# Three steps of a single-core FNet and ReGLU kernel moved later, and the first rounding of a transform block given to GpSimd

## The chip, the core and the metric

The kernel runs on one core of a Trainium2 chip. The core has five engines with a queue of instructions each: TensorE (PE, with its weight loads shown apart as PEld), VectorE (DVE), ScalarE (ACT), GpSimd (POOL) and SyncE (SP, which here only issues transfers). They meet through semaphores. The metric is the device time of one execution in microseconds (us). Before the change it is 1030.93 us, the median of 3 runs (1029.65 to 1031.65).

## What is computed

`x` is 2048 tokens by 640 features. The rows are normalized, and the result is the sum of the input, a two-dimensional Fourier transform of the normalized rows (its real part, by matrices) and a gated feed-forward layer with 1728 hidden units:

```python
xn = _layernorm(x, axis=-1)
# A: Fourier mixing
a = jnp.einsum("bsd,ed->bse", xn, dft_hid_re)
b = jnp.einsum("bsd,ed->bse", xn, dft_hid_im)
A = jnp.einsum("ts,bse->bte", dft_seq_re, a) - jnp.einsum("ts,bse->bte", dft_seq_im, b)
# B: gated layer
gate = jnp.einsum("bsd,df->bsf", xn, W_gate)
up = jnp.einsum("bsd,df->bsf", xn, W_up)
h = gate * (gate > 0) * up
B = jnp.einsum("bsf,fd->bsd", h, W_down)
return x + A + B
```

## The kernel before

**Products.** Every float32 operand is split in two parts that TensorE can take at its full rate: a rounded high part and a low remainder. The high part is a copy with a rounding output type, mostly made by ScalarE; the low part is the operand minus its high part, made by VectorE or GpSimd (`split`, L123 to L125). A product of two operands is three matmuls of 128x128 weights by 512 columns: high by high, high by low, low by high (`mm3`, L130 to L132). Where a block scheme with 7 products in place of 8 can be used, sums and differences of blocks are formed first; this is what names such as B11, T1 or S2 stand for.

**Stages.** The first stage (to about 400 us) normalizes the tokens and multiplies them by the sequence transform, whose blocks of 128x1024 stream in from memory. The second (405 to 722 us by its first and last weights) computes the gate and the up projection. The third multiplies by the hidden transform and by `W_down`, adds the input and stores (`project`).

**Work lists.** The first and the third stage are lists of units, each with four steps: load, prepare, run and finish. `drive(4, 2)` walks over the list and issues, at step i, the preparation of unit i-2, the load of unit i, the finish of unit i-5 and the matmuls of unit i-4. The order in which an engine gets its instructions follows from this walk and from a scheduler; instructions that pass through `pin` keep the order of the program. Each queue runs strictly in order, so an instruction that waits holds up all that stands behind it on its engine.

**The start.** A token group is 256 tokens, two to a partition (j = 0 and 1). `first_group` (L287) does group 0 by halves so that TensorE can begin early. 48 small matmuls on zeros (L112) keep TensorE busy while data arrive. The transfer of the x rows of j = 0 comes first, then the transform block `raw` of column chunk c = 0, then that of c = 1. VectorE takes mean and variance (L204, L205), ScalarE the square root (L210), VectorE its inverse (L210). `high(0, 0)` (L303, recorded at L292) is the ScalarE copy that rounds the first 128x512 block of `raw` into `cb`. Then come the high parts of the normalized tokens, columns 0 to 127 first (L231), and VectorE's low parts (L235). `behind_vector` (L248) is a one-column GpSimd multiply that reads the last of VectorE's low parts; it only puts GpSimd's next step behind it in time. That step, `low(0, 0, nc.gpsimd)` (L293), is the low part of the first `raw` block.

`first_products` (L502 on, recorded at L510) issues the matmuls of group 0 in this order for each j: high by high for c = 0, the tokens' low parts for c = 0, both for c = 1, and at the end the matmuls that take the low parts of the transform, c = 0 ahead of c = 1. So 12 matmuls stand ahead of the first one that needs GpSimd's L293.

**The other groups.** `next_group` (L250) does groups 1 to 7. For groups 1 to 3 its last VectorE step scales the columns that are kept in float32 (L276, two instructions), and `keep_a21` has GpSimd's queue store them. In the list, the split of the transform block for c = 1 of the running group is recorded right behind (L570, at L124 and L125), held there by `issue_after`. For group 4 (g equal to NH), ScalarE rounds both token halves (L231), and then copies three accumulators out of PSUM (`keep_first`, L593 on, at L121), which frees the next matmuls of chunk 0.

**The third stage's loads.** `get_y` (L1206) loads the blocks of x to which the results are added. `project` records it behind the unit u = 3 of each product; for B11 it loads three blocks (L1211) on SP's queue, between the loads of units 3 and 4.

Of the kernel before, what the change touches and what calls it, by code (L numbers as in the profile page):

```python
# [10 lines left out]
OP = mybir.AluOpType  # L11
# [8 lines left out]
SG = 2  # L20
# [38 lines left out]
def fnet_reglu_kernel(  # L59
# [43 lines left out]

    root_t = keep.tile([P, 1], F32, name="root_t")
    nc.scalar.activation(root_t, eps_t, AF.Sqrt)

    warm = keep.tile([P, P], mybir.dt.bfloat16, name="warm")
    nc.vector.memset(warm, 0.0)
# [121 lines left out]
    def ln_high(g, xs, mv, j, cs):  # L230
        return nc.scalar.activation(ln_parts(g, j, cs)[0], xs[:, j, cs], AF.Copy, scale=mv[:, j, 4:5])  # L231
# [10 lines left out]
    def pin(steps):  # L242
        return [tc.keep_in_program_order(i) for i in steps]
# [6 lines left out]
    def next_group(g, b, raw, before):  # L250

        xs, bs, mv = ln_tiles(g)
        js = slice(0, SG)
        cs = K14 if g < NH else slice(0, D)
        low = lambda engine, j: pin([engine.tensor_tensor(flat(b, 1)[:, j], raw[:, j], flat(b, 0)[:, j].bitcast(F32), op=OP.subtract)])
        pin(ln_stats(g, xs, bs, mv, js))
        pin([nc.scalar.activation(flat(b, 0), raw, AF.Copy)])
        if before is not None:
            behind_vector(before)
            for j in range(SG):  # L260
                low(nc.gpsimd, slice(j * CH, (j + 1) * CH))
        root, inverse = ln_first(g, mv, js)
        pin([root])
        pin([ln_mean(g, mv, js)])
        pin([ln_center(xs, mv, 0, cs)])
        pin([inverse()])
        pin([ln_high(g, xs, mv, 0, cs)])
        pin([ln_center(xs, mv, 1, cs)])
        late["high"] = pin([ln_high(g, xs, mv, 1, cs)])[0].ins
        if before is None:  # L270
            for j in range(SG):
                low(nc.vector, slice(j * CH, (j + 1) * CH))
        pin(ln_refine(g, mv, js))
        late["ln"] = pin(ln_low(g, xs, j, cs) for j in range(SG))[-1].ins
        if g < NH:
            late["ln"] = pin(nc.vector.tensor_scalar(xs[:, j, K2], xs[:, j, K2], mv[:, j, 0:1], stat[:, 1, g, j : j + 1],  # L276
                                                     op0=OP.subtract, op1=OP.mult) for j in range(SG))[-1].ins
            keep_a21(g)
        if g == NG - 1:
            nc.sync.dma_start(rows.rearrange("m (g p j) -> p m g j", p=P, j=SG), stat)  # L280
        if g == 2:
            st = stage()[:, :CH].rearrange("p (j d) -> p j d", j=SG)
            for j in range(SG):
                late["high"] = pin([nc.scalar.activation(st[:, j], ln_place(0)[:, j, K2], AF.Copy, scale=stat[:, 1, 0, j : j + 1])])[0].ins
            keep_a21(0, st)

    def first_group(b):  # L287


        xs, bs, mv = ln_tiles(0)  # L290
        part = lambda c, j: b[c][1][:, j * CH : (j + 1) * CH]
        high = lambda c, j: pin([nc.scalar.activation(b[c][0][:, 0, j], part(c, j), AF.Copy)])  # L292
        low = lambda c, j, engine: pin([engine.tensor_tensor(b[c][0][:, 1, j], part(c, j), b[c][0][:, 0, j].bitcast(F32),  # L293
                                                             op=OP.subtract)])
        d0, d14 = slice(0, P), slice(P, 3 * P)
        last = lambda j: ln_parts(0, j, K14)[1][:, 3 * P - 1 :]
        j0, j1 = slice(0, 1), slice(1, 2)
        pin(ln_stats(0, xs, bs, mv, j0))
        root, inverse = ln_first(0, mv, j0)
        pin([root])  # L300
        pin([ln_center(xs, mv, 0, d0)])
        pin([inverse()])
        high(0, 0)  # L303
        pin([ln_high(0, xs, mv, 0, d0)])
        pin([ln_center(xs, mv, 0, d14)])
        pin([ln_high(0, xs, mv, 0, d14)])
        pin(ln_refine(0, mv, j0))
        high(1, 0)
        pin(ln_low(0, xs, 0, cs) for cs in (d0, d14))
        behind_vector(last(0))  # L310
        low(0, 0, nc.gpsimd)

        low(1, 0, nc.vector)
        pin(ln_stats(0, xs, bs, mv, j1))
        high(0, 1)
        root, inverse = ln_first(0, mv, j1)
        pin([root])
        pin([ln_center(xs, mv, 1, K14)])
        pin([inverse()])
        pin([ln_high(0, xs, mv, 1, K14)])  # L320
        pin(ln_refine(0, mv, j1))
        high(1, 1)
        pin([ln_low(0, xs, 1, K14)])
        behind_vector(last(1))
        low(0, 1, nc.gpsimd)
        low(1, 1, nc.gpsimd)
        pin([ln_mean(0, mv, slice(0, SG))])
        for j in range(SG):
            pin([nc.scalar.activation(xs[:, j, K2], xs[:, j, K2], AF.Identity, bias=stat[:, 0, 0, j : j + 1])])
# [203 lines left out]
    def first_stream(c, name, g):  # L533

        t = {}
        half = int(name == "B21")
        n = half * NH + g

        norm = {0: 0 if n == 0 else None, 1: n + 1 if n < NG - 1 else None}.get(c)

        def load():
            if n == 0 and c == 0:
                st = start["raw"] = [raw(), raw()]
                get = lambda c, j: nc.sync.dma_start(st[c][:, j * CH : (j + 1) * CH], dft[c, 0, 0][:, j * CH : (j + 1) * CH])
                ln_load(0, slice(0, 1))
                get(0, 0)
                get(1, 0)
                ln_load(0, slice(1, 2))
                get(0, 1)
                get(1, 1)  # L550
                return
            if norm is not None:
                tc.keep_in_program_order(ln_load(norm, slice(0, SG)))
            if n > 0 or c > 1:
                t["s"] = raw()
                nc.sync.dma_start(t["s"], dft[c, 0, n])
                start[c, n] = t

        def prepare():
            if norm == 0:  # L560
                start["b"] = [(parts(), st) for st in start["raw"]]
                first_group(start["b"])
                return
            if (n > 0 or c > 1) and "b" not in t:
                t["b"] = b = parts()
                with ExitStack() as order:
                    if c == 1:
                        order.enter_context(tc.issue_after(late["ln"]))
                        order.enter_context(tc.issue_after(late["high"]))
                    i = split(flat(b, 0), flat(b, 1), t["s"])  # L570
                if c == 1 and n < NG - 1:
                    late["ln"] = i.ins
            if norm is not None:
                t1 = start[0, norm]
                t1["b"] = parts()
                next_group(norm, t1["b"], t1["s"], flat(b, 1)[:, W2 - 1 : W2] if norm > 1 else None)

        def run():
            if n == 0 and c < 2:
                first_products(c, start["b"])  # L580
                return
            if n > 0 and c == 0:
                next_products(n, t["b"])
                if n == NH - 1:
                    keep_first()
                return
            accs = [(c, ("e1", i)) for i in range(2)]
            with ExitStack() as order:
                if n > 0 and c == 1:
                    order.enter_context(tc.issue_after(start["pe"]))  # L590
                product(g, t["b"], resident(n, 0), accs, half == 0, half == 1, ((c, "v1"), half, half == 0))

        def keep_first():  # L593
            t["first"] = sums_a()
            for i, key in enumerate((("e1", 0), ("e1", 1), "v1")):
                pin([copy(t["first"][:, i], E[c, key])])

        def finish():
            if g == NH - 1:
                s = t.get("first")  # L600
                if s is None:
                    s = (sums_a, sums_b)[c % 2]()
                    for i, key in enumerate((("e1", 0), ("e1", 1), "v1")):
                        copy(s[:, i], E[c, key])
                defer(1, lambda: nc.gpsimd.dma_start(pqd[c][0][:, :3] if half else firsts[c], s[:, :3]))

        todo.append((load, prepare, run, finish))
# [451 lines left out]
    def project(q):  # L1059
# [184 lines left out]
        for name in ("B11", "T1", "B21", "T2", "B22", "T3", "T4"):  # L1244
# [4 lines left out]
            for u in range(len(units)):  # L1249
                l, p, r = unit(name, u, u == 0)  # L1250
                end = u == len(units) - 1 and not (tiles and name != "T3")
                todo.append((l, p, r, (lambda name: lambda: read(name))(name) if end else idle))
                if u == 3:
                    todo.append(((lambda name: lambda: get_y(name))(name), idle, idle, idle))
                if name == "B21" and u in (0, 2):
                    (plain_rest if u else plain_block)()
# [50 lines left out]
```

## Time and profile before

| | |
|---|---|
| median of 3 runs | 1030.93 us |
| time of the profiled execution | 1030.23 us |
| its span, first to last instruction | 1028.3 us |
| VectorE busy | 805.9 us, 78% |
| ScalarE busy | 427.6 us, 42% |
| GpSimd busy | 118.1 us, 11% |
| memory traffic | 242.73 MB, 236 GB/s |

The profile is one execution. Its span is 1.9 us shorter than the time of the same execution, and that time is 0.7 us below the median. In a row, `L123` is a line of the kernel, `out<-in` gives the names of the buffers, `xN` is a number of instructions, and a bracket at the end says how long the engine had been idle before it and what ended the wait. An engine's name with a q (`SPq`, `POOLq`) is its sequencer. A matmul's end is modelled by the profiler, so the pace of TensorE is read from the starts.

### The profile page before, as it was taken

What the parts mean: (1) busy time and instruction counts of PE and PEld (TensorE: products, weight loads), DVE (VectorE), ACT (ScalarE), POOL (GpSimd) and SP (SyncE); (2) the same over time, 40 slices, a digit from 0 to 9 for tenths busy, and PEclk for the clock granted to TensorE, in tenths of its full rate; (3) what the DMA queues carried; (4) which work ended last, traced back from release to release, by engine and by line L of the source; (5) the groups of instructions that cost most, each with busy time, mean ns of one, the idle gap of its engine ahead of it and who ended that gap; (6) DMA issues with size and microseconds to landing.
All of it is one profiled execution on the core that took longest, in us unless ns stands there. A gap on an engine that the chain in (4) does not pass through costs nothing.

```text
span 1028.3 us, 12486 instructions
## 1 busy us (share of the span) xinstructions
PE 1022.1 (99%) x4528; PEld 844.5 (82%) x4528; DVE 805.9 (78%) x1089; ACT 427.6 (42%) x534; POOL 118.1 (11%) x184
## 2 busy tenths in 40 slices
PE   9999999999999999999999999999999999999998
PEld 7888888888888888888888888888888888888886
DVE  8967987998989586788878988886597666886764
ACT  5554453343433333433335443443355423552531
POOL 3431001012110002411110001000000000000000
PEclk9999999999999999999999999999999999999999
DMA  7987734968969785763474665662699647986543
GB/s 304 342 278 274 265 124 164 338 221 262 349 229 348 299 323 165 249 213 136 153 237 152 225 228 216 230 255 103 237 346 302 189 132 232 357 322 213 156 154 122
DMA packets 101469, 242.73 MB, mean 236 GB/s; under 512 B 11552, under 2 KB 50976, under 8 KB 98848
## 3 DMA queue, kind: packets, MB, share of 16 engines
q1 hardware_dynamic: 83664, 171.68, 48.6%
q0 software_dynamic: 17744, 70.26, 18.6%
q8 instruction: 35, 0.57, 0.2%
q14 instruction: 26, 0.21, 0.1%
HBM read 182.12 MB, written 58.74 MB: 234 GB/s over the span
## 4 chain that ended last, share of the span: by engine, by line
PE 98%; DMA 1%; DVE 0%; SPq 0%; ACT 0%; issue 0%; DVEq 0%
PE ps L132 31%; PE ps L131 31%; PE ps L130 31%; PE ps L481 3%; PE ps L1204 1%; PE ps L510 1%; DMA rw<-hd 1%; DMA r<-in_x 0%; SPq L1211 0%; DVE wt L125 0%; DVE bs L204 0%; DVE y L1214 0%; ACT cb L292 0%; SPq L1100 0%; SPq L1071 0%
## 5 line engine op out<-in xcount | busy, mean ns | idle before, releaser
L132 PE MATMUL ps<-cb,wt 128*128 128x512 f32 x390 | 151.9, 390 | 0.4 <-DVE wt L125 0.4
L130 PE MATMUL ps<-cb,wt 128*128 128x512 f32 x390 | 151.8, 389 | 0.0
L131 PE MATMUL ps<-cb,wt 128*128 128x512 f32 x390 | 151.7, 389 | 0.0
L125 DVE TENSOR_TENSOR cb<-rw,cb 128x1024 fp32r<-128x1024 f32 x83 | 94.0, 1132 | 68.4 <-ACT cb L124 66.9
L124 ACT ACTIVATE cb<-rw 128x1024 fp32r<-128x1024 f32 x83 | 82.0, 988 | 147.3 <-PE ps L132 127.6
L124 ACT ACTIVATE cb<-raw 128x1024 fp32r<-128x1024 f32 x71 | 75.3, 1060 | 114.2 <-PE ps L132 107.8
L125 DVE TENSOR_TENSOR cb<-raw,cb 128x1024 fp32r<-128x1024 f32 x71 | 86.8, 1222 | 40.3 <-ACT cb L124 40.1
L132 PE MATMUL ps<-xs_early,gw 128*128 128x512 f32 x260 | 101.2, 389 | 0.0
L131 PE MATMUL ps<-xs_early,gw 128*128 128x512 f32 x260 | 101.2, 389 | 0.0
L130 PE MATMUL ps<-xs_early,gw 128*128 128x512 f32 x260 | 101.1, 389 | 0.0
L130 PE MATMUL ps<-cb,xs_late 128*128 128x512 f32 x232 | 90.2, 389 | 0.0
L131 PE MATMUL ps<-cb,xs_late 128*128 128x512 f32 x232 | 90.2, 389 | 0.0
L132 PE MATMUL ps<-cb,xs_late 128*128 128x512 f32 x232 | 90.2, 389 | 0.0
L121 ACT ACTIVATE gw<-z 128x1024 fp32r<-128x1024 f32 (+1 forms) x52 | 57.6, 1109 | 76.4 <-DVE z L814 76.4
L131 PE MATMUL ps<-cb,xs_early 128*128 128x512 f32 x226 | 88.0, 390 | 0.0
L132 PE MATMUL ps<-cb,xs_early 128*128 128x512 f32 x226 | 87.9, 389 | 0.0
L130 PE MATMUL ps<-cb,xs_early 128*128 128x512 f32 x226 | 87.9, 389 | 0.0
L132 PEld LDWEIGHTS ps<-cb,wt 128*128 128x128 f32 x390 | 73.2, 188 | 16.0 <-DVE wt L125 0.7
L131 PEld LDWEIGHTS ps<-cb,wt 128*128 128x128 f32 x390 | 73.2, 188 | 15.4
L130 PEld LDWEIGHTS ps<-cb,wt 128*128 128x128 f32 x390 | 73.2, 188 | 15.2
L121 ACT ACTIVATE u<-ps 128x512 f32<-128x512 f32 x52 | 31.1, 597 | 94.0 <-PE ps L132 94.0
L824 DVE TENSOR_TENSOR gw<-z,gw 128x1024 fp32r<-128x1024 f32 (+1 forms) x52 | 64.6, 1283 | 3.8 <-ACT gw L121 3.8
(190 smaller groups left out, 1983.1 us busy)
## 6 DMA issues: line engine op xcount, KB each, us to landing
raw<-in_dft SPq DMA_DIRECT2D x94, 512.0 KB, 5.5
wt<-wparts SPq DMA_DIRECT2D x66, 256.0 KB, 3.2
z<-in_wgu SPq DMA_DIRECT2D x26, 640.0 KB, 4.0
hd<-ob POOLq DMA_DIRECT2D x26, 512.0 KB, 3.7
rw<-hd SPq DMA_DIRECT2D x24, 512.0 KB, 6.4
wparts<-pw POOLq DMA_DIRECT2D x11, 1024.0 KB, 4.1
tk<-in_dft SPq DMA_DIRECT2D x16, 512.0 KB, 6.1
set<-r POOLq DMA_DIRECT2D x16, 512.0 KB, 4.0
```

What stands on the lines that cost most here:

```text
L121: return nc.scalar.activation(o, i, AF.Copy)
L124: nc.scalar.activation(hi, src, AF.Copy)
L125: return nc.vector.tensor_tensor(lo, src, hi.bitcast(F32), op=OP.subtract)
L130: nc.tensor.matmul(ps, wh, mh, start=first, stop=False, skip_group_check=more)
L131: nc.tensor.matmul(ps, wh, ml, start=False, stop=False, skip_group_check=more)
L132: nc.tensor.matmul(ps, wl, mh, start=False, stop=last, skip_group_check=more)
L481: start["pe"] = pin([nc.tensor.matmul(E[0, key], xn_part(n * SG + j, d)[v == 1], b[:, int(v == 2), j], start=False, stop=n % NH == NH - 1 ...
L510: pin([nc.tensor.matmul(E[c, key], xn_part(j, d)[v == 1], b[c][0][:, int(v == 2), j], start=j == 0 and v == 0, stop=False)])
L824: tt(self.w[:, 1, cs], self.z[:, cs], self.w[:, 0, cs].bitcast(F32), op=OP.subtract)
L1204: nc.tensor.matmul(B[key], wr[:, v, es], hr[:, cs], start=False, stop=v == 1, skip_group_check=not new)
```

## The change

The diff makes five edits.

```diff
@@ kernel, ahead of the work lists
     nc.scalar.activation(root_t, eps_t, AF.Sqrt)
+    nc.gpsimd.tensor_copy(root_t, eps_t)
...
@@ next_group
-        late["high"] = pin([ln_high(g, xs, mv, 1, cs)])[0].ins
+        if g != NH:
+            late["high"] = pin([ln_high(g, xs, mv, 1, cs)])[0].ins
...
-        late["ln"] = pin(ln_low(g, xs, j, cs) for j in range(SG))[-1].ins
+        late["ln"] = pin(ln_low(g, xs, j, cs) for j in range(SG)[: 1 if g == NH else SG])[-1].ins
+        if g == NH:
+
+            def second():
+                late["high"] = pin([ln_high(g, xs, mv, 1, cs)])[0].ins
+                late["ln"] = pin([ln_low(g, xs, 1, cs)])[0].ins
+
+            late["second"] = second
         if g < NH:
-            late["ln"] = pin(nc.vector.tensor_scalar(xs[:, j, K2], xs[:, j, K2], mv[:, j, 0:1], stat[:, 1, g, j : j + 1],
-                                                     op0=OP.subtract, op1=OP.mult) for j in range(SG))[-1].ins
-            keep_a21(g)
+            late["a21"] = g, xs, mv
...
+    def scale_a21():
+
+        if "a21" not in late:
+            return
+        g, xs, mv = late.pop("a21")
+        late["ln"] = pin(nc.vector.tensor_scalar(xs[:, j, K2], xs[:, j, K2], mv[:, j, 0:1], stat[:, 1, g, j : j + 1],
+                                                 op0=OP.subtract, op1=OP.mult) for j in range(SG))[-1].ins
+        keep_a21(g)
@@ first_group
-        high(0, 0)
+        pin([nc.gpsimd.tensor_copy(b[0][0][:, 0, 0], part(0, 0))])
@@ first_stream, prepare
                 if c == 1 and n < NG - 1:
                     late["ln"] = i.ins
+                    scale_a21()
@@ first_stream, keep_first
                 pin([copy(t["first"][:, i], E[c, key])])
+            late["second"]()
@@ project
-                if u == 3:
+                if u == (len(units) - 1 if (name, q) == ("B11", 1) else 3):
                     todo.append(((lambda name: lambda: get_y(name))(name), idle, idle, idle))
```

- VectorE's scaling of the kept columns (groups 1 to 3), and with it the store of `keep_a21`, stands behind the split for c = 1 instead of ahead of it.
- For group 4 the second token half is rounded by ScalarE behind the three PSUM copies instead of ahead of them, and its low part by VectorE follows.
- The three loads of `get_y` for B11 in the first call of `project` (q = 1) stand behind unit 5 instead of unit 3.
- The first block of `raw` is rounded by a GpSimd copy, and ScalarE loses one instruction of 128x512.
- A one-column GpSimd copy into `root_t` is added; it waits for the ScalarE square root that writes the same tile.

The matmuls and their order are the same in both programs. On VectorE only the two scaling instructions of three groups change places with a split, and the adds of the B11 results with their neighbours. On SP the loads of the x rows of groups 4 to 7 each stand behind two more loads of transform blocks than before.

One more thing changes place. In the program before, GpSimd's queue begins, behind four small memsets, with an instruction of its own kind that reloads the library of its code (MODIFY_POOL_CONFIG in the trace, two records on its sequencer). The builder puts it directly ahead of the first instruction that needs that library, which is the multiply of `behind_vector` (L248). Copies do not need it, so the program after reads: the one-column copy, the copy of the `raw` block (which waits for the block's transfer), the library reload, the multiply of `behind_vector`, the low part of the first block.

## The prediction

> **What bounds the kernel now.** I read the busy times of the page first, then TensorE's waits, then the chain of waits from the start, and last the single matmuls around each stall.
>
> ```profile
> PE 1022.1 (99%) x4528; PEld 844.5 (82%) x4528; DVE 805.9 (78%) x1089; ACT 427.6 (42%) x534; POOL 118.1 (11%) x184
> ```
>
> ```profile
> PE ps L112 <- DVE warm L108: 1.0, 1, 1.0
> PE ps L510 <- ACT xs_early L231: 0.6, 1, 0.6
> PE ps L132 <- DVE wt L125: 0.4, 1, 0.4
> ```
>
> TensorE is busy for 1022 of 1028 us and waits three times, for 2.0 us in all. An edit elsewhere can therefore gain very little, and any delay that reaches TensorE is paid in full. The chain of the first 20 us shows what lets it start:
>
> ```profile
> 3.68 0.90 DVE bs L204 x2
> ...
> 5.04 0.61 ACT cb L292
> 5.65 0.30 ACT xs_early L231
> ...
> 6.00 8.78 PE ps L510 x36
> 14.78 4.09 PE ps L481 x18
> ```
>
> ScalarE's rounding of the first block (5.04 to 5.65) and of the first token columns set the first real matmul at 6.00. Undisturbed, 18 matmuls take 4.09 us, 0.227 us each. A start later than that after its predecessor is lost time, even where no wait is listed, because the modelled matmul ends hide it. The timeline of TensorE shows three such places that the moves touch:
>
> ```profile
> 18.71 0.39 PE L130 MATMUL ps<-cb,xs_early 128*128 128x512 f32 x1
> 19.06 0.50 PE L131 MATMUL ps<-cb,xs_early 128*128 128x512 f32 x1
> 19.40 0.40 PE L132 MATMUL ps<-cb,xs_early 128*128 128x512 f32 x1
> ...
> 39.37 1.80 PE L481 MATMUL ps<-cb,xs_late 128*128 128x512 f32 x6
> ...
> 745.34 0.39 PE L131 MATMUL ps<-cb,wt 128*128 128x512 f32 x1
> 746.08 0.50 PE L132 MATMUL ps<-cb,wt 128*128 128x512 f32 x1 [0.35 <-DVE wt L125]
> 746.42 0.40 PE L130 MATMUL ps<-cb,wt 128*128 128x512 f32 x1
> ```
>
> At 18.71 two intervals take 0.69 instead of 0.45 us: 0.24 lost. At 39.37 five intervals take 1.80 less the last matmul's 0.39, so 1.41 instead of 1.13: 0.28 lost. At 745.34 two take 1.08 instead of 0.45: 0.63 lost. Together 1.15 us. That is all the three moves can recover at these places.
>
> **The three moves.** What stands in the way at each place:
>
> ```profile
> 17.14 0.73 DVE L276 TENSOR_SCALAR r<-r,mv,stat 128x256 f32<-128x256 f32 x2
> 17.79 1.22 DVE L125 TENSOR_TENSOR cb<-raw,cb 128x1024 fp32r<-128x1024 f32 x1
> ...
> 36.79 1.55 ACT L231 ACTIVATE xs_late<-r,mv 128x640 fp32r<-128x640 f32 x2 [0.83 <-DVE mv L210]
> 38.37 1.57 ACT L121 ACTIVATE sa<-ps 128x512 f32<-128x512 f32 x3
> ...
> 735.10 1.29 SPq L1211 DMA_DIRECT2D y<-in_xt  x3
> 736.44 0.43 SPq L1071 DMA_DIRECT2D rw<-hd  x1
> ```
>
> The low part that ends at 19.01 releases the matmul of 19.06. With the two scalings (0.65 us of issue, 17.14 to 17.79) behind it, it ends before 18.4, and the 0.24 us go. The three PSUM copies of 38.37 start up to 0.78 us earlier with half of L231 behind them, more than the 0.28 lost. The load for unit 4 is issued 1.34 us earlier (736.44 less 735.10), more than the 0.63. I take all 1.15 us; the bounds are 0 and 1.15. What is now later: GpSimd's store of the kept columns, by the 1.14 us of a split, and the x rows of groups 4 to 7, behind two more transform loads.
>
> ```profile
> 24.07 0.80 SPq L199 DMA_DIRECT2D r<-in_x  x2
> ```
>
> ```profile
> r<-in_x SPq DMA_DIRECT2D x1, 640.0 KB, 4.3
> ```
>
> ```profile
> 33.41 0.88 DVE L204 BATCH_NORM_STATS2 bs<-r 128x6 f32<-128x320 f32 x2
> ```
>
> The first of them (issued at 24.07) lands at 28.4, and its statistics start at 33.41, so 5 us cover it. Two more issues ahead (0.38 to 0.40 us each), and their data, fit. If that cover went, the statistics would push VectorE's lows and TensorE with them, up to the excess. The moved y loads come out of the issue ahead of units 4 and 5, and lie far ahead of their adds, which follow the product's last unit. All of this costs nothing.
>
> **The first block on GpSimd.** Two things must be priced: the copy itself, and the library reload that now stands behind it. First when the copy can start, and what TensorE's first matmul needs besides:
>
> ```profile
> raw<-in_dft SPq DMA_DIRECT2D x1, 256.0 KB, 3.1
> ```
>
> ```profile
> 1.19 0.89 SPq L544 DMA_DIRECT2D raw<-in_dft  x2
> ...
> 5.17 0.16 DVE L210 RECIPROCAL mv<-mv 128x1 f32<-128x1 f32 x1
> ...
> 5.56 0.79 ACT L231 ACTIVATE xs_early<-r,mv 128x128 fp32r<-128x128 f32 x2
> ...
> 6.35 0.75 DVE L235 SCALAR_TENSOR_TENSOR xs_early<-r,stat,xs_early 128x128 fp32r<-128x128 f32 x2
> ```
>
> The block lands at 1.19 + 3.1 = 4.3. Freed of its copy, ScalarE could start on the token columns when the inverse is there (5.33) instead of at 5.56, so TensorE could start at about 5.8 instead of 6.0. The one-column copy ahead waits only for ScalarE's square root, before 2.3, and costs nothing. Now GpSimd, whose rows before are these (the first is from the view of the line L248):
>
> ```profile
> L248 POOLq MODIFY_POOL_CONFIG  x2: 8/10/11, 0.7 to 0.8; - x2
> ```
>
> ```profile
> 7.19 0.57 POOL L248 TENSOR_TENSOR root_t<-xs_early 128x1 f32<-128x1 f32 x1 [6.74 <-DVE xs_early L235]
> 7.71 1.28 POOL L293 TENSOR_TENSOR cb<-raw,cb 128x512 fp32r<-128x512 f32 x1
> 10.80 0.19 POOL L248 TENSOR_TENSOR root_t<-xs_early 128x1 f32<-128x1 f32 x1 [1.80 <-DVE xs_early L235]
> 10.94 2.54 POOL L293 TENSOR_TENSOR cb<-raw,cb 128x512 fp32r<-128x512 f32 x2
> ```
>
> The trace has no GpSimd copy. From below its price is the 0.19 us of a one-column instruction, from above the 1.28 us of the two-input instruction of the same size. I take 1.28, the row of the same size: the copy runs from 4.3 to 5.6, ScalarE's own ended at 5.65, and TensorE could start at 5.8.
>
> The reload is issued at 0.7 to 0.8 before the change and has no row of its own length. Its end is bounded by the first instruction that needs it: the multiply of 7.19 was released by VectorE (6.35 + 0.75), and took 0.57 us where the next took 0.19. If these 0.38 us are the rest of the reload, it ended at 7.57 and took 6.8 us; if they are something else, it took anything from 0 to 6.4. I take 6.8, because the surplus is there once, at the first instruction that needs the library, and nothing else marks the end. In the program before, this lies under the wait for the data. Behind the copy nothing covers it: 5.6 + 6.8 = 12.4. Then comes the multiply (0.14 to the next start, 10.80 to 10.94) and L293 (1.28), which ends at 13.8 instead of 9.0.
>
> Who waits for it:
>
> ```profile
> 9.05 0.53 PEld L510 LDWEIGHTS ps<-cb,xs_early 128*128 128x128 f32 x3 [0.20 <-POOL cb L293]
> ```
>
> The 13th matmul's weight load already waits for GpSimd, so it has no slack at all. TensorE does its first 12 matmuls (3.05 us from 6.00) by about 8.9, then stands still, and resumes 4.8 us later than before. Queued behind on GpSimd are the low parts of the other half blocks (10.94), which hold their `raw` buffers, and the loads that refill these on SP; they shift by no more than TensorE, whose next use of each comes after the resumption. Since a reload under heavier traffic can last longer, I set an upper bound from these rows:
>
> ```profile
> 1.02:4.24 3.22, 3.21 (x31) 1.00 0.78 236
> 4.24:5.28 1.04, 1.04 (x20) 1.00 0.75 148
> 6.00:9.39 3.39, 3.39 (x13) 1.00 1.04 413
> ```
>
> The columns are TensorE's busy time and matmuls, the granted clock, the DMA share and GB/s. The share is 0.78 while the old reload ran and 1.04 where the new one will: 6.8 times 1.04/0.78 is 9.1 us, an estimate, and the shift would be 7.1.
>
> The Trainium skill, GPSIMD Engine Reference, section 2.1, says the first call to freshly loaded code pays about 6 us (5.95 measured) with no instruction to be seen in the profile. The trace agrees as far as it can: no row shows the load, and 6.8 is its most. With 5.95 the shift would be 4.0, and the time below would be 0.9 us less.
>
> **The slow array.** The same rows show a second cost: the small matmuls take 0.104 us each in the first 3.22 us (x31) and 0.052 after that (x20), although the clock column gives 1.00 for both. An array that has stood still runs at half speed for about 3.2 us, which costs 1.6 us. The pause of 0.6 us at 5.4 brings no such loss. The new pause is 5.0 us (8.9 to 13.9). The bounds are 0 and 1.6; I take 1.6, since the pause is much nearer to standing still than to 0.6 us.
>
> The Trainium skill, TensorE: Matmul & The Clock Gate, Part 1, says that the gate falls to half speed after an idle window of about 3.4 us and reopens after a busy one. That gives about 1.7 us here. No run here shows the fall after a pause.
>
> **Sum.** The reload behind the copy +4.8, the slow array +1.6, the moves -1.15: +5.25 us. The earlier start (-0.2) drops out, since the wait for GpSimd absorbs it. On the profiled execution's 1030.23 this is 1035.5. That run is 0.7 us below the median of the runs shown, so I predict 1036.2.
>
> **Rivals.**
> (a) Not slower: the reload is short, or already done when the multiply needs it. GpSimd then loses nothing as long as the reload takes less than about 2.0 us behind the copy (9.0 less 1.4 less 5.6). The start gains 0.2, the moves 1.15: 1030.9 - 1.35 = 1029.6. For it: no row gives the length. Against it: the surplus of 0.38 us.
> (b) The reload runs beside the copy. GpSimd's sequencer could pass the reload on while the copy still waits for its block, from about 2.3 us, behind the one-column copy. It ends at 9.1, L293 at 10.5, the shift is 1.5 us, the pause too short to slow the array: 1030.9 + 1.5 - 1.15 = 1031.3. Against it: the queue is in order, and a wait holds what stands behind it.
> (c) The copy does not do what it is for. If a GpSimd copy took twice the two-input time (2.6 us), the block would be ready at 6.9, and the first matmul would come at about 7.1 instead of 6.0. With a short reload: 1030.9 + 1.1 - 1.15 = 1030.9. With the long one the shift grows by 1.3.
> (d) The reload lasts 9.1 us under the transfers: 2.3 more than forecast, 1038.5.
>
> **How the numbers follow.** About 0.2% (2.1 us) is what a measurement of this kernel can tell from no change. Forecast with its own spread 0.55 (1033.5 to 1037.5), (d) or a longer copy with the long reload 0.17, (a) 0.12, (b) 0.10, (c) alone 0.06. Range: the high end is (d) plus a copy longer by 1.3, 1039.8. The low end lies between (a) and (b), at 1031, where a reload of about 4 us without a slow array (shift 2.0, less 1.15: 1031.8) is inside; (a) and (c) are left out below. Slower by over 0.2%, above 1033.0: forecast and (d), 0.72. Within: (b), (c) and most of (a), 0.22. Faster, below 1028.9: the rest of (a), 0.06, since all the gains together are 1.35.
>
> **What would show it.** In the profile after, the two configuration records should stand behind a GpSimd copy at about 5.6; L249 (the old L248) should start or end near 12.4, and the first L309 (the old L293) end near 13.8; TensorE should show a new wait of about 5 us <-POOL on its first-products line, and intervals of about 0.45 us for some 3 us behind it. The losses at 18.7, 39.4 and 745 should be gone. If the first GpSimd subtraction still ends near 9, the step about the reload is wrong, and (a) holds. If it ends near 10.5, it is (b).

## The result and the profile after

The changed kernel takes 1032.69 us, the median of 22 runs (1032.48 to 1034.81), beside 1030.93 us for 22 runs of the kernel before. The ratio is 1.0020 with a 95% interval of 1.0013 to 1.0026: slower by 1.8 us. The profiled execution took 1032.51 us and its span is 1030.5 us, 2.2 us more than the span before.

In the program after, the lines have moved: L131 to L133 are the old L130 to L132, L226 the old L225 (VectorE centers the tokens, that is, it subtracts the mean), L232 the old L231, L241 the old L240, L249 the old L248, L256 the old L255, L309 the old L293, L497 and L526 the old L481 and L510. L122 is the old L121 (the copies out of PSUM), L299 is the scaling that was L276, and L319 is the new GpSimd copy. In the kernels of the experiments the numbers shift again by a few lines; operation and tile names tell which step a row is.

The busy times of the page after:

```profile
PE 1022.8 (99%) x4528; PEld 844.7 (82%) x4528; DVE 808.9 (78%) x1089; ACT 426.1 (41%) x533; POOL 118.8 (12%) x186
```

VectorE executes the same 1089 instructions as before, and is busy 3.0 us longer (808.9 for 805.9). Some of its instructions have become longer; which ones, the timeline must tell. TensorE's waits after (total, times, longest):

```profile
PE ps L497 <- ACT xs_early L232: 1.4, 2, 1.0
PE ps L113 <- DVE warm L109: 1.0, 1, 1.0
PE ps L497 <- ACT sa L122: 0.7, 1, 0.7
PE ps L526 <- ACT xs_early L232: 0.4, 1, 0.4
```

The wait of 5 us for GpSimd that was forecast isn't there. New are two waits for the high parts of a token group (L232) and one for a copy out of PSUM (L122). The timeline of TensorE after, at the places that the prediction named and at the new ones:

```profile
18.78 0.39 PE L131 MATMUL ps<-cb,xs_early 128*128 128x512 f32 x1
19.01 0.39 PE L132 MATMUL ps<-cb,xs_early 128*128 128x512 f32 x1
...
22.64 0.39 PE L133 MATMUL ps<-cb,xs_early 128*128 128x512 f32 x1
24.00 0.96 PE L497 MATMUL ps<-cb,xs_early 128*128 128x512 f32 x3 [0.97 <-ACT xs_early L232]
...
32.06 0.39 PE L133 MATMUL ps<-cb,xs_early 128*128 128x512 f32 x1
32.85 1.43 PE L497 MATMUL ps<-cb,xs_early 128*128 128x512 f32 x5 [0.39 <-ACT xs_early L232]
...
40.91 0.39 PE L133 MATMUL ps<-cb,xs_early 128*128 128x512 f32 x1
42.01 2.18 PE L497 MATMUL ps<-cb,xs_late 128*128 128x512 f32 x6 [0.71 <-ACT sa L122]
...
745.34 0.39 PE L131 MATMUL ps<-cb,wt 128*128 128x512 f32 x1
745.57 0.39 PE L132 MATMUL ps<-cb,wt 128*128 128x512 f32 x1
```

At 18.78 and 745.34 the next start follows after 0.23 us: these two losses are gone. At 22.64 the next start comes 1.36 us later where 0.227 is normal, and the two intervals in the row behind it take 0.96 - 0.39 = 0.57 where 0.45 is normal: 1.25 lost. The same sum gives 0.69 at 32.06 and 1.53 at 40.91, which takes the place of the old loss at 39.37. Before, the first of these places, the change from one token group to the next, was free:

```profile
22.82 0.39 PE L132 MATMUL ps<-cb,xs_early 128*128 128x512 f32 x1
23.05 1.75 PE L481 MATMUL ps<-cb,xs_early 128*128 128x512 f32 x7
```

| lost by TensorE, us | before | after |
|---|---|---|
| 18.7 | 0.24 | 0 |
| 22.6 (group 2 begins) | 0 | 1.25 |
| 32.1 (group 3 begins) | 0 | 0.69 |
| 39.4 before, 40.9 after (group 4 begins) | 0.28 | 1.53 |
| 745.3 | 0.63 | 0 |
| sum | 1.15 | 3.47 |

The difference is 2.3 us, and the spans differ by 2.2. So this table is the whole change. The first block and the library reload don't appear in it.

**The first block.** GpSimd's timeline after, where the bracket gives the idle time and what ended it:

```profile
4.54 0.61 POOL L319 CAST cb<-raw 128x512 fp32r<-128x512 f32 x1 [2.05 <-DMA raw<-in_dft]
7.31 0.50 POOL L249 TENSOR_TENSOR root_t<-xs_early 128x1 f32<-128x1 f32 x1 [2.16 <-DVE xs_early L236]
7.76 1.29 POOL L309 TENSOR_TENSOR cb<-raw,cb 128x512 fp32r<-128x512 f32 x1
...
19.39 0.89 POOL L241 DMA_DIRECT2D xs_early<-r  x1 [5.84 <-DVE r L299]
20.30 0.20 POOL L249 TENSOR_TENSOR root_t<-cb 128x1 f32<-128x1 f32 x1
20.45 2.54 POOL L256 TENSOR_TENSOR cb<-raw,cb 128x512 fp32r<-128x512 f32 x2
...
37.51 2.53 POOL L256 TENSOR_TENSOR cb<-raw,cb 128x512 fp32r<-128x512 f32 x2
```

The copy takes 0.61 us, as ScalarE's did, and is done at 5.15. The reload now stands behind it, and yet the multiply starts at 7.31, released by VectorE as before (7.19), and the subtraction ends at 9.05 for 8.99. An end near 9 is what the prediction named as the sign that its step about the reload is wrong. TensorE's first matmul comes at 5.96 for 6.00. This edit moves nothing by more than about 0.1 us.

**The new losses.** The rows from 19.39 to 20.45 show where they begin. The store of the kept columns is issued at 19.39 and holds GpSimd for 0.89 us; the two low parts of the next transform block stand behind it and run from 20.45 to 22.99. The same stretch of GpSimd before:

```profile
18.20 0.88 POOL L240 DMA_DIRECT2D xs_early<-r  x1 [4.72 <-DVE r L276]
19.11 0.20 POOL L248 TENSOR_TENSOR root_t<-cb 128x1 f32<-128x1 f32 x1
19.25 2.54 POOL L255 TENSOR_TENSOR cb<-raw,cb 128x512 fp32r<-128x512 f32 x2
```

There the store's issue lay beside VectorE's split, which ends at 19.01 and for which the multiply had to wait anyway. It cost nothing, and the low parts ran from 19.25 to 21.79, 1.2 us earlier. In the program after, the split is done sooner, at 18.42, but the multiply can't use that: it stands behind the store, and the store waits for the scaling, which now comes after the split. VectorE's timeline after:

```profile
7.07 0.68 DVE L309 TENSOR_TENSOR cb<-raw,cb 128x512 fp32r<-128x512 f32 x1
...
21.02 2.20 DVE L226 TENSOR_SCALAR r<-r,mv 128x384 f32<-128x384 f32 x1
...
30.05 2.02 DVE L226 TENSOR_SCALAR r<-r,mv 128x384 f32<-128x384 f32 x1
...
38.12 2.28 DVE L226 TENSOR_SCALAR r<-r,mv 128x640 f32<-128x640 f32 x1
```

And the same three centerings before:

```profile
20.96 1.06 DVE L225 TENSOR_SCALAR r<-r,mv 128x384 f32<-128x384 f32 x1
...
28.28 1.11 DVE L225 TENSOR_SCALAR r<-r,mv 128x384 f32<-128x384 f32 x1
...
35.45 1.23 DVE L225 TENSOR_SCALAR r<-r,mv 128x640 f32<-128x640 f32 x1
```

Here are VectorE's 3.0 us: 1.14 + 0.91 + 1.05 = 3.1 in three instructions. In both programs the first centering starts at nearly the same time, and ends 0.23 us behind GpSimd's second subtraction: 22.02 for 21.79 before, 23.22 for 22.99 after. In group 4 after, the subtractions end at 40.04 and the centering at 40.40. It seems unable to run while GpSimd subtracts. The delay is in no list of waits, since the instruction counts as busy all along. ScalarE's high part of the group (L232) needs the centered tokens and starts at 23.33, and TensorE stands still until 24.00.

### The profile page after: what moved, and what is told of

It reads as the page before. It is cut to its first block, busy times and chain, and to the rows that moved or that the text cites. A ratio compares the mean times of both kernels' runs of the same rounds, so it can differ in the third digit from the quotient of the medians.

```text
span 1030.5 us, 12486 instructions
## 1 busy us (share of the span) xinstructions
PE 1022.8 (99%) x4528; PEld 844.7 (82%) x4528; DVE 808.9 (78%) x1089; ACT 426.1 (41%) x533; POOL 118.8 (12%) x186
## 4 chain that ended last, share of the span: by engine, by line
PE 96%; DVE 3%; ACT 0%; DMA 0%; issue 0%; DVEq 0%; ACTq 0%
PE ps L133 31%; PE ps L131 31%; PE ps L132 31%; PE ps L497 2%; PE ps L1222 1%; DVE r L226 1%; DVE bs L205 1%; DVE cb L126 0%; DMA r<-in_x 0%; DVE xs_early L236 0%; DVE mv L206 0%; DVE r L299 0%; DVE cb L256 0%; ACT cb L125 0%; ACT xs_early L232 0%
## 5 line engine op out<-in xcount | busy, mean ns | idle before, releaser
L133 PE MATMUL ps<-cb,wt 128*128 128x512 f32 x390 | 151.8, 389 | 0.0
L131 PE MATMUL ps<-cb,wt 128*128 128x512 f32 x390 | 151.8, 389 | 0.0
L132 PE MATMUL ps<-cb,wt 128*128 128x512 f32 x390 | 151.7, 389 | 0.0
L132 PE MATMUL ps<-xs_early,gw 128*128 128x512 f32 x260 | 101.2, 389 | 0.0
L131 PE MATMUL ps<-xs_early,gw 128*128 128x512 f32 x260 | 101.2, 389 | 0.0
L133 PE MATMUL ps<-xs_early,gw 128*128 128x512 f32 x260 | 101.2, 389 | 0.0
L132 PE MATMUL ps<-cb,xs_late 128*128 128x512 f32 x232 | 90.3, 389 | 0.0
L131 PE MATMUL ps<-cb,xs_late 128*128 128x512 f32 x232 | 90.3, 389 | 0.0
L133 PE MATMUL ps<-cb,xs_late 128*128 128x512 f32 x232 | 90.3, 389 | 0.0
L122 ACT ACTIVATE gw<-z 128x1024 fp32r<-128x1024 f32 (+1 forms) x52 | 57.6, 1109 | 76.4 <-DVE z L832 76.4
L132 PE MATMUL ps<-cb,xs_early 128*128 128x512 f32 x226 | 87.9, 389 | 0.0
L133 PE MATMUL ps<-cb,xs_early 128*128 128x512 f32 x226 | 87.9, 389 | 0.0
L131 PE MATMUL ps<-cb,xs_early 128*128 128x512 f32 x226 | 87.9, 389 | 0.0
L132 PEld LDWEIGHTS ps<-cb,wt 128*128 128x128 f32 x390 | 73.2, 188 | 15.4
L133 PEld LDWEIGHTS ps<-cb,wt 128*128 128x128 f32 x390 | 73.2, 188 | 15.3
L131 PEld LDWEIGHTS ps<-cb,wt 128*128 128x128 f32 x390 | 73.2, 188 | 15.1
L122 ACT ACTIVATE u<-ps 128x512 f32<-128x512 f32 x52 | 31.0, 597 | 94.7 <-PE ps L133 94.7
```

Source lines behind the costliest of these rows:

```text
L122: return nc.scalar.activation(o, i, AF.Copy)
L131: nc.tensor.matmul(ps, wh, mh, start=first, stop=False, skip_group_check=more)
L132: nc.tensor.matmul(ps, wh, ml, start=False, stop=False, skip_group_check=more)
L133: nc.tensor.matmul(ps, wl, mh, start=False, stop=last, skip_group_check=more)
```

## Experiments

Each kernel was timed against the kernel before on the same chip; losses are read as in the table above. Four theories stand against each other, by the letters that the expectations use. **R**: the library reload behind the copy costs time, and the moves by themselves give up to the 1.15 us that the prediction took. **P**: the loss comes with the moved store, which delays GpSimd's subtractions, and these lock VectorE's centering out. **M**: the second half of group 4, behind the PSUM copies, is what hurts. **S**: the scaling itself, in its new place ahead of the statistics, delays VectorE.

**1. The first block alone.** The kernel before with the two GpSimd copies:

```diff
     nc.scalar.activation(root_t, eps_t, AF.Sqrt)
+    nc.gpsimd.tensor_copy(root_t, eps_t)
...
-        high(0, 0)
+        pin([nc.gpsimd.tensor_copy(b[0][0][:, 0, 0], part(0, 0))])
```

> The kernel before with the first-block edit alone (the GpSimd copies, and with them the library reload behind them). Theory P (the loss comes from GpSimd's later low parts, which hold back VectorE's centering in groups 2 to 4): this edit is close to nothing, within 0.3 us of the kernel before; first matmul at about 5.96, the 13th at about 9.15, GpSimd's first multiply near 7.3 as in the kernel after. Theory R (the reload behind the copy costs time): slower by 1.8 us or more, with TensorE waiting for GpSimd.

Measured: 1030.78 us for 1031.35, ratio 0.9994 [0.9985, 1.0003]. The edit costs nothing that can be seen, and gains nothing. The first half of theory R falls. The span of this profile is 1.2 us longer than that of the kernel before, and TensorE's timeline shows all of that in one other place:

```profile
744.98 0.39 PE L133 MATMUL ps<-cb,wt 128*128 128x512 f32 x1
745.92 0.50 PE L131 MATMUL ps<-cb,wt 128*128 128x512 f32 x1 [0.56 <-ACT wt L125]
...
747.32 0.50 PE L133 MATMUL ps<-cb,wt 128*128 128x512 f32 x1 [0.38 <-DVE wt L126]
747.66 0.40 PE L131 MATMUL ps<-cb,wt 128*128 128x512 f32 x1
```

Four intervals take 2.68 us where 0.91 is normal: 1.77 lost, where the profile of the kernel before lost 0.63. This is the place that the moved loads of `get_y` relieve, and its size varies between profiles of kernels that are the same there.

**2. The moves alone.** The changed kernel without the first-block edit:

```diff
-    nc.gpsimd.tensor_copy(root_t, eps_t)
...
-        pin([nc.gpsimd.tensor_copy(b[0][0][:, 0, 0], part(0, 0))])
+        high(0, 0)
```

> The kernel after without the first-block edit: the three moves alone. Theory P: slower than before by 1.5 to 2.4 us, as the whole change, with losses of TensorE near 22.6, 32 and 41 us of 1.2, 0.7 and 1.5 us. Theory R: faster than before by up to 1.15 us, the sum that the prediction gave the moves.

Measured: 1033.04 us for 1031.35, ratio 1.0018 [1.0009, 1.0026], the loss of the whole change. The centerings take 2.19, 2.01 and 2.29 us, and the losses at 22.6, 32 and 41 are there. The other half of theory R falls: the moves together cost time.

**3. Only the scaling and its store moved.** The kernel before with this part of the diff:

```diff
-            late["ln"] = pin(nc.vector.tensor_scalar(...))[-1].ins
-            keep_a21(g)
+            late["a21"] = g, xs, mv
...
                     late["ln"] = i.ins
+                    scale_a21()
```

> The kernel before with the scaling of the kept columns (and the store on GpSimd's queue) behind the split, nothing else. Theory P: slower than before by 2.4 to 3.2 us (the change's loss plus the 0.63 us at 745 that this kernel does not get back, the 41 us place uncertain); VectorE's centering of 128x384 takes about 2 us in groups 2 and 3. Rival M (the second half of group 4 behind the PSUM copies is what hurts): faster by about 0.2 us, no long centering.

Measured: 1036.56 us for 1031.35, ratio 1.0049 [1.0036, 1.0061]. That is 5.2 us, more than the 2.4 to 3.2 that P forecast. The centerings of groups 2 and 3 take 2.20 and 2.01 us although group 4's second half has not moved, which M does not allow. TensorE's waits:

```profile
PE ps L488 <- ACT sa L121: 1.4, 1, 1.4
PE ps L488 <- ACT xs_early L231: 1.4, 2, 1.0
...
PE ps L130 <- ACT ob L121: 0.9, 1, 0.9
```

The second row is P's loss, 1.24 and 0.67 us at 22.8 and 32.2. At 41 it grows to 2.2 (first row), since here the PSUM copies still stand behind both token halves: the delayed first half pushes the second, and this pushes the copies. The third row, 1.2 us at 454.7, isn't P's: ScalarE's copy into `ob` waited there for a store that was issued at 446.0 and landed at 455.3. Why this store is late in this kernel alone was not tried. With 1.2 us at 750 the losses sum to 6.5; less the 1.15 of before this is 5.4, and 5.2 were measured.

**4. The other two moves alone.** The kernel before with the second token half of group 4 behind the PSUM copies, and the loads of `get_y` behind unit 5:

```diff
+            late["second"]()
...
-                if u == 3:
+                if u == (len(units) - 1 if (name, q) == ("B11", 1) else 3):
```

> The kernel before with the two other moves: the second half of group 4 behind the PSUM copies, and the y loads behind unit 5. Theory P: faster than before by 0.6 to 0.9 us (0.63 at 745 and up to 0.28 at 39.4); the centering stays at 1.1 us. Rival M: slower, with a loss above 1 us near 40 us.

Measured: 1029.47 us for 1031.35, ratio 0.9981 [0.9971, 0.9991]: faster, where M forecast a slower kernel. The centerings take 1.06, 1.11 and 1.24, as before, and the start of group 4 is free in TensorE's timeline (eight intervals in 2.20 - 0.39 = 1.81 us, 0.226 each):

```profile
39.74 0.39 PE L132 MATMUL ps<-cb,xs_early 128*128 128x512 f32 x1
39.97 2.20 PE L489 MATMUL ps<-cb,xs_late 128*128 128x512 f32 x9
```

It gains 1.9 us by the medians, more than the 0.6 to 0.9 forecast, where the profile of the kernel before lost 0.91 at these two places. That the place at 745 varies (0.63 in one profile, 1.77 in another) would account for the rest; no run measures it by itself.

**5. The store behind the low parts.** The changed kernel, where only the store is held back until the next group's subtractions have been issued on GpSimd:

```diff
             for j in range(SG):
                 low(nc.gpsimd, slice(j * CH, (j + 1) * CH))
+            if "store" in late:
+                keep_a21(late.pop("store"))
...
-        keep_a21(g)
+        late["store"] = g
```

> The kernel after, with the store of the kept columns issued on GpSimd's queue behind the next group's two low parts instead of ahead of them; the scaling on VectorE stays behind the split. Theory P: GpSimd's low parts of group 2 start near 18.6 instead of 20.5 and end near 21.1, so the first centering of 128x384 takes about 0.5 us instead of 2.2; the losses near 22.6 and 32 us go and the one near 41 shrinks below 0.5; faster than the kernel before by 0.7 to 1.5 us (about 1029.9). Rival S (the scaling itself, in its new place ahead of the statistics, delays VectorE): still slower than before, with the losses near 22.6 and 32 us at 0.5 us or more.

Measured: 1030.07 us for 1030.74, ratio 0.9997 [0.9988, 1.0006]. The losses at 22.6 and 32 are gone, and so is the slowdown, though the scaling still stands in its new place: theory S falls. But the gain that was forecast is missing, and 0.7 us are lost at the start of group 4. VectorE's timeline tells why:

```profile
28.81 0.67 DVE L226 TENSOR_SCALAR r<-r,mv 128x384 f32<-128x384 f32 x1
...
35.77 2.12 DVE L226 TENSOR_SCALAR r<-r,mv 128x640 f32<-128x640 f32 x1
```

and GpSimd's:

```profile
34.24 0.73 POOL L241 DMA_DIRECT2D xs_early<-r  x1 [0.69 <-DVE r L301]
35.00 2.54 POOL L256 TENSOR_TENSOR cb<-raw,cb 128x512 fp32r<-128x512 f32 x2
```

For group 3's store the scheduler kept the old order: it stands ahead of the subtractions (34.24), they end at 37.54, and the centering of group 4 takes 2.12 us. Where the store stands behind, as in group 3, the subtractions end at 29.26 and the centering of 28.81 takes 0.67. One program shows both cases, though the experiment did not do all that it was meant to.

**6. The subtractions after the centerings.** The changed kernel with GpSimd's low parts of groups 2 to 7 held until VectorE's second centering is done:

```diff
-        if before is not None:
-            behind_vector(before)
-            for j in range(SG):
-                low(nc.gpsimd, slice(j * CH, (j + 1) * CH))
...
         pin([ln_center(xs, mv, 1, cs)])
+        if before is not None:
+            behind_vector(xs[:, 1, cs][:, -1:])
+            for j in range(SG):
+                low(nc.gpsimd, slice(j * CH, (j + 1) * CH))
```

> The kernel after, with GpSimd's one-column multiply and the two low parts of groups 2 to 7 held until VectorE's second centering is done (the multiply reads that centering's last column). Theory P: no centering of 128x384 meets a GpSimd subtraction, so both take 0.4 to 0.5 us (2.2 and 0.4 before), although the scaling and the store stand where the change put them; GpSimd's low parts end later, near 25, and may become a wait of TensorE of their own. Rival S (place of the scaling) or traffic of the store: the first centering stays at 1 us or more.

Measured: 1033.25 us for 1030.74, ratio 1.0023 [1.0014, 1.0032]. VectorE's timeline:

```profile
21.02 0.37 DVE L226 TENSOR_SCALAR r<-r,mv 128x384 f32<-128x384 f32 x1
...
38.60 0.50 DVE L226 TENSOR_SCALAR r<-r,mv 128x640 f32<-128x640 f32 x1
```

With GpSimd silent beside it, the instruction that took 2.20 us takes 0.37, and the one that took 2.28 takes 0.50. That is P's claim at its plainest, and it clears the store's own transfer too, since the store stands where the change put it. As a remedy it is no good: the subtractions now come so late that TensorE waits for them.

```profile
PE ps L497 <- ACT sa L122: 0.6, 1, 0.6
PE ps L497 <- POOL cb L256: 0.3, 1, 0.3
```

They also hold up VectorE in another place. GpSimd's subtractions of group 2 now run from 22.25 to 24.80, beside two small steps with two inputs each, which take 0.16 us in the changed kernel:

```profile
22.26 1.30 DVE L221 TENSOR_TENSOR mv<-mv 128x2 f32<-128x2 f32 x1
23.59 1.23 DVE L222 SCALAR_TENSOR_TENSOR stat<-mv 128x2 f32<-128x2 f32 x1
```

Each lasts as long as one subtraction, and the tokens' low parts stand behind them. Not every VectorE instruction is held: in the kernel before, two statistics instructions (L204) ran at 19.96 inside the subtractions of 19.25 to 21.79 and took 0.83 us, the same as here, where GpSimd subtracts nothing at that time.

**7. The change without the scaling move.** First-block edit and the other two moves, with scaling and store where they were:

```diff
-            late["a21"] = g, xs, mv
+            late["ln"] = pin(nc.vector.tensor_scalar(...))[-1].ins
+            keep_a21(g)
...
-                    scale_a21()
```

> The kernel after without the move of the scaling: the first-block edit, the second half of group 4, and the y loads. Theory P: faster than the kernel before by 0.7 to 1.2 us, as the two moves alone, centerings at 1.1 us. Theory R (the first-block edit costs): not faster.

Measured: 1029.29 us for 1030.74, ratio 0.9986 [0.9977, 0.9995]. One step less, and the change is faster than the kernel before, by 1.45 us where 0.7 to 1.2 were forecast; as in experiment 4, the place at 745 may account for the rest. TensorE waits only once in its span, for the zeros at the start.

**8. The subtraction right behind the reload.** The changed kernel without the first `behind_vector`, one run and a profile:

```diff
-        behind_vector(last(0))
         low(0, 0, nc.gpsimd)
```

> The kernel after without the first one-column multiply, so that the first low part stands directly behind the library reload and waits for nothing else. It shows the reload's length: if the reload takes 6.8 us as predicted, the low part ends near 13; if it is done within the 2.2 us that the kernel after leaves it, the low part starts or ends so that it is over by 8.8; without any cost it starts near 5.2 and is over by 6.7.

This measures the reload by itself. The view of the line L309 shows the two records of the reload (nanoseconds, then first and last start), and GpSimd's timeline what runs around them:

```profile
L309 POOLq MODIFY_POOL_CONFIG  x2: 7/9/11, 5.1 to 5.1; - x2
```

```profile
4.52 0.61 POOL L319 CAST cb<-raw 128x512 fp32r<-128x512 f32 x1 [2.04 <-DMA raw<-in_dft]
5.21 1.27 POOL L309 TENSOR_TENSOR cb<-raw,cb 128x512 fp32r<-128x512 f32 x1
```

The copy ends at 5.13, the records stand at 5.1, and an instruction that needs the library starts at 5.21 and takes its usual 1.27 us. The reload costs 0.1 us at most. The run took 1033.97 us, and its beginning shows P's lock once more in VectorE's timeline:

```profile
5.36 1.28 DVE L226 TENSOR_SCALAR r<-r,mv 128x256 f32<-128x256 f32 x1
```

This centering took 0.34 us in the changed kernel, where GpSimd did nothing at that time. Here it ends at 6.64, behind the subtraction's 6.48, and the second of TensorE's first products comes at 7.23, 1.21 us behind the first one. That is about the 1.3 us by which this one run is longer than the changed kernel's median.

**9. All stores behind the low parts.** Experiment 5 with the store's place pinned:

```diff
-        nc.gpsimd.dma_start(xn_block(g, K2, 0).bitcast(F32), ...)
+        pin([nc.gpsimd.dma_start(xn_block(g, K2, 0).bitcast(F32), ...)])
```

> The kernel with the store behind GpSimd's low parts, and the stores held in program order, so that the store of group 3 also stands behind the low parts of group 4 (the scheduler had put it ahead of them). Theory P: the centering of 128x640 near 35.8 us falls from 2.12 to below 1.0, the loss near 39 to 41 us from 0.7 to below 0.4, and the time is 1.0 to 1.4 us below the kernel before. Rival (the second half of group 4 behind the PSUM copies causes that loss): centering shorter, loss near 39 to 41 stays at 0.6 or more.

Measured: 1029.24 us for 1030.97, ratio 0.9989 [0.9980, 0.9997]: 1.7 us faster where 1.0 to 1.4 were forecast, with the shortest span of all, 1027.1. GpSimd's and VectorE's timelines:

```profile
33.22 2.72 POOL L256 TENSOR_TENSOR cb<-raw,cb 128x512 fp32r<-128x512 f32 x2
35.88 0.75 POOL L241 DMA_DIRECT2D xs_early<-r  x1
```

```profile
35.48 0.81 DVE L226 TENSOR_SCALAR r<-r,mv 128x640 f32<-128x640 f32 x1
```

Now the store stands behind in all three groups, the subtractions end at 35.94 (40.04 in the changed kernel, 37.54 in experiment 5), the centering of group 4 takes 0.81 for 2.28, and no loss of TensorE is left at the three places. Group 4's second half is still behind the PSUM copies, so M has nothing left to explain. The scaling is still behind the split, so it was never the scaling itself that cost time, but the store on GpSimd's queue that went with it. Beside experiment 7, in another batch, no difference can be told.

## Why the prediction was right and wrong

**The direction was right by luck, the reason wrong.** Forecast was 5.25 us slower, from a reload and a slow array, less 1.15 for the moves. It came out 1.8 slower, from a step that the prediction called free.

**The reload (+4.8) is the first step that failed.** The prediction took the multiply's surplus, 0.57 us where the next took 0.19, for the rest of a reload of 6.8 us. Experiment 8 gives the reload 0.1 us at most, and the same library's first instruction there has no surplus. What the surplus was, the VectorE row of the profile after tells: its subtraction L309 with two inputs ran from 7.07 to 7.75, and GpSimd's multiply of 7.31 ended at 7.81. In the kernel before, they ended at 7.70 and 7.76. In both the multiply ends 0.06 us behind the VectorE instruction beside it, which looks like the same lock with the roles exchanged. The prediction had allowed for "something else", with anything from 0 to 6.4 for the reload, and took 6.8 because the surplus appears only once, without comparing the multiply's end with the ends on VectorE. The Trainium skill, GPSIMD Engine Reference, section 2.1, gives about 6 us for the first call to freshly loaded code; the trace does not agree here, with 0.1 us between the records and the first instruction behind them. Why no load shows, for instance whether the code was in place already, no run here tells.

**The slow array (+1.6)** was to follow from the pause behind the reload, and fell with it. No run here has such a pause, so whether the array would have slowed is open.

**The copy** was taken at 1.28, its upper bound, and took 0.61. The rival of a slow copy falls. The 0.2 us that TensorE was to start earlier shrank to 0.04: ScalarE began its token columns at 5.42 for 5.56, and the first matmul waits for these, not for the copy. From one profile to the next this start varies by more: 5.96 to 6.08 in the kernels with the copy, 6.00 to 6.20 in those without.

**The moves (-1.15) are the second step that failed.** The places and their sizes were right, and experiments 4 and 7 recover them. The moves of group 4's second half and of the `get_y` loads do what was forecast; the x rows behind two more loads cost nothing, as forecast. But the scaling move was priced at the 0.24 us that it frees on VectorE. Of the store that goes with it, the prediction said that it comes later by 1.14 us and left it at that. What stands behind the store on GpSimd's queue was not followed, though it is two rows further down in the same timeline: a multiply and two subtractions. They now wait until the scaling ahead of the store is done, and then through the store's issue of 0.89 us: they begin at 20.30, where in experiment 9, with the store behind them, the multiply begins at 18.50. The price was 3.47 us of new losses for 0.24.

**Why a delay of GpSimd reaches TensorE.** The centering does not run beside GpSimd's subtractions (experiments 6, 8 and 9 against 2 and 5). The Trainium skill, SBUF — State Buffer, section "Who interferes with whom", says that VectorE and GpSimd share a pair of ports as an exclusive lock, held for a whole instruction, and names `tensor_scalar` among the operations that can take it. The trace agrees: 2.20 us beside the subtractions, 0.37 without. What it shows beyond is that VectorE waited for both subtractions, one right behind the other, and not only for the one that was running.

**The rivals.** Rival (a), a short reload, had the right premise, and its 1029.6 failed by the same unpriced store; experiment 7, where the store stays in place, comes to 1029.29. Rival (b) supposed a reload of the same length, (c) a slow copy, (d) a longer reload: none of these occurs.

## What to carry to other kernels

When a step is moved, its transfers move too: follow what stands behind each of them on the queue that issues it, and who waits for that, before the step is called free. An instruction that takes several times its usual time, with no wait listed, may be waiting for another engine inside its own duration; compare its end with the ends on the other engines before a cause is put to it. A surplus that appears once is better looked for in the rows that end with it than in an event that has no row.

## What the runs showed of the hardware

A reload of GpSimd's library, with an instruction that needs it right behind, cost 0.1 us at most. A GpSimd copy of 128x512 took 0.61 us, as long as ScalarE's, and less than half of GpSimd's two-input subtraction of that size (1.27 to 1.30). A VectorE `TENSOR_SCALAR` of 128x384 took 0.37 us alone, and 2.20 us when it began during the first of two GpSimd subtractions that stood back to back: it ended 0.23 us behind the second. Two-input VectorE instructions of 128x2, 0.16 us alone, took 1.30 and 1.23 us beside such subtractions, while statistics of 128x320 took the same time beside them as without.
